# Routing tail and first expert tiles of a chunked-attention and top-2 expert kernel: tile order, copy engines and one-hots rearranged

## The chip, the cores and the metric

The kernel runs on one core of a Trainium2 chip. Its time is the device time of one execution in microseconds (us); a median of several runs stands for it. A core has TensorE (PE: matmuls, and transposes done as matmuls), VectorE (DVE), ScalarE (ACT), GpSimd (POOL) and SyncE (SP). The last two mostly issue DMAs here. The profiler records one execution; "PEld" are TensorE's weight loads, which run beside its matmuls.

## The reference

Attention over chunks of 32 positions, with 16 positions of context to the left, 8 to the right and 8 memory rows, feeds a mixture of 8 experts, of which each token takes its best two.

```python
# q, k, v: (4, 8, 768, 64); mem_k, mem_v: (4, 8, 8, 64)
for c in range(S // 32):
    k_full = concat(mem_k, k[max(0, c0 - 16):min(S, c1 + 8)])
    a = softmax(q[c0:c1] @ k_full.T / 8)
    out[c0:c1] = a @ v_full
x = out as (3072, 512)
noisy = x @ w_gate + log1p(exp(x @ w_noise)) * noise      # (3072, 8)
top2 = the two largest; weights = softmax over these two
out = sum over the two experts e: weight * (relu(x @ w1[e]) @ w2[e])   # F = 1024
```

## The kernel before

The 3072 tokens are 24 groups of 128 (six for each batch). The kernel has three stages.

**Attention** goes batch by batch, two groups at a time: twelve steps `i` (`NT = 12`, `TP = 3` for each batch). Step `i` issues the scores of step `i + 1` (`scores`, L408), turns its own probabilities by TensorE (`turn_p`), multiplies by the values (`values`), turns the result (`turn_x`) and multiplies it by the gate weights (`gate`, L489). `gate` leaves 16 logits for each token in one PSUM tile, `small`, from where they are copied into `lg_all` (L496). Between two batches the queries and keys of the next are turned in eight units of two heads (`turns`, L560). The plan `KS`/`QS` (L570) says for each unit which engine copies PSUM to SBUF: a key unit is two copies, and the unit's number tells how many of the two go to ScalarE, the others going to VectorE. While TensorE would wait, `warm` (L450) gives it matmuls whose results nobody reads.

**Routing** runs beside it in four parts of groups: `r0` (0 to 5), `ra` (6 to 13), `rb` (14 to 19) and `rc` (20 to 23), each an object of `Route` (L239). `noise` makes the noise scale on ScalarE. `choose` is a chain of 14 short VectorE steps that finds the two best experts and ends in `ohp`, a one-hot over the 28 pairs of experts. `ranks` counts by matmul how many earlier tokens have the same pair: a triangle within the group, and matrices of ones for earlier groups and for the running total `cum` of the earlier parts. `place` reads the rank of each token (`ohr`, `rank`), `total` adds the part's counts to `cum` (L330, L334), and `slots` makes the one-hot `oh_l` of the rank over 128 places (L341). `weights` and `values` prepare the facts of each token on GpSimd, and `lists` brings them by matmul to the place of their pair and rank. `decode` then gives `src`, the row to be gathered for each place of each pair.

**Experts**: the rows of each pair form a tile of 128. `gathers` fetches tiles by indirect DMA (L695) into six buffers, in blocks of six or eight tiles. They are turned by TensorE for the first block (`turn_slots`, L715) and by DMA on SP's queue for the others (`turn_dma`, L720). `mm1` multiplies by `w1` (L738) and leaves the relu to ScalarE and VectorE in turn, `mm2` multiplies by `w2` (L752), and the weighted sum goes to the output by indirect DMA. The loads of the experts' weights stand on the same GpSimd queue as the gathers, in the order of the program.

In the attention and routing stage the order on TensorE, ScalarE, VectorE and SP is that of the program (`manual_schedule`), and so it is for TensorE and VectorE at the opening of the expert stage. Everything emitted later is put in by a planner, which may place an instruction between two of those. Waits between engines are derived from tiles; two engines do not read the same PSUM bank of one tile at the same time.

The first step of the expert stage takes three tiles for expert 0. Before, the first of them goes alone, so that TensorE can begin when one tile has landed, and the other two are a pair:

```python
h0 = mm1(xTs[b][:, :, 0:1, :], 1, static_w(e), 0, others)   # others: turn tiles 1 and 2
s0, n = 1, 2
h = mm1(xTs[b][:, :, s0:s0 + (n - 1) * ds_ + 1:ds_, :], n, static_w(e), i % 2)
```

Of the kernel before, what the change touches and what calls it, by code (L numbers as in the profile page):

```python
# [11 lines left out]
F32 = mybir.dt.float32  # L12
# [3 lines left out]
Alu = mybir.AluOpType  # L16
# [6 lines left out]
def kernel(  # L23
# [215 lines left out]
    class Route:  # L239
# [10 lines left out]

        def noise(self):
            self.ns = self.tile("ns", E).rearrange("p (n e) -> p n e", e=E)
            nc.scalar.activation(out=self.ns, in_=self.lg[:, :, E:2 * E], func=Act.Exp)
            nc.scalar.activation(out=self.ns, in_=self.ns, func=Act.Ln, bias=1.0)
# [35 lines left out]

        def ranks(self):
            n, M = self.n, self.M
            self.p_rank = bank([128, n, NP], F32, name="p_rank")
            nc.tensor.matmul(out=self.p_rank, lhsT=tri, rhs=M, start=True, stop=False)
            nc.tensor.matmul(out=self.p_rank, lhsT=ones, rhs=cum[-1].unsqueeze(1).to_broadcast([128, n, NP]),
                             start=False, stop=False)
# [17 lines left out]

        def settle(self):
            yield from self.place()
            yield from self.total()
            self.slots(nc.vector)
            yield
# [16 lines left out]

        def slots(self, eng, parts=1):
            n = self.n // parts
            self.oh_l = self.tile("oh_l", 128, BF16).rearrange("p (n t) -> p n t", t=128)
            for g in range(0, self.n, n):  # L340
                keep_order(eng, eng.tensor_tensor(out=self.oh_l[:, g:g + n], in0=bc(self.rr[:, g:g + n], 128),  # L341
                                                  in1=io_l.unsqueeze(1).to_broadcast([128, n, 128]), op=Alu.is_equal))

# [145 lines left out]
    def gate(t, xT):  # L489
        b, tp = divmod(t, TP)  # L490
        ps_l = small[:, 2 + t % 2, 0:4 * E].rearrange("p (j e) -> p j e", j=2)
        for j in range(2):
            for kp in range(KP):
                nc.tensor.matmul(out=ps_l[:, j, :], lhsT=xT[:, kp, j, :], rhs=wgn[:, kp, :],
                                 start=(kp == 0), stop=(kp == KP - 1))
        nc.vector.tensor_copy(lg_all[:, 2 * t:2 * t + 2, :], ps_l)  # L496

# [32 lines left out]
    with tc.manual_schedule(engines={ET.PE, ET.Activation, ET.DVE, ET.SP}):  # L530
# [38 lines left out]

        KS = ((0, 2), (1, 0), (2, 2), (3, 2))  # L570
        QS = ((4, 1), (5, 1), (6, 1), (7, 1))
# [4 lines left out]
        for i in range(NT):  # L576
# [24 lines left out]
            if tp == TP - 1 and more:  # L601
                home = psO.tile([128, 2, HP, 2, D], F32, name="ps_o")
                waits = lambda pair: warm(home[:, 0].rearrange("p c a d -> p (c a d)"), (0, 4, 0, 1)[pair])
            if not last:
# [19 lines left out]
            if i in (TP + 2, 2 * TP + 2):  # L624
                advance((ra if b > 1 else r0).settle())
            if i in (2 * TP, 3 * TP):
# [7 lines left out]
            if i == 2 * TP + 1:  # L634
                ra.noise()
                advance(ra.choose())
            if i == NT - 2:
                rb.noise()
                chosen = rb.choose()
                advance(chosen, 7)  # L640
            fill(i, 2)

        i = NT - 1
# [159 lines left out]
    wl = next(dec)  # L803
    advance(rc.total())

# [148 lines left out]
    for i, (b, e, s0, ds_, n, ps_) in enumerate(steps):  # L954
        if i == 0:
# [4 lines left out]
            nc.vector.tensor_copy(xTs[0][:, :, 6, :], xTs[0][:, :, 0, :])  # L960
            s0, n = 1, 2
        h = mm1(xTs[b][:, :, s0:s0 + (n - 1) * ds_ + 1:ds_, :], n, static_w(e), i % 2)
        if i == 0:
            turn_slots(0, 3, 1)
            turn_slots(0, 4, 2)
            turn_block(1, 0, 8)
            opening.close()
        if prev is not None:
            second(prev, held=held if i == len(steps) - 1 else None)
        for f in feed.get(i, ()):  # L970
            f()
        tiles = []
# [4 lines left out]
        if i == 0:  # L977
            second((h0, 1, static_w(e), tiles[0:1]))
            tiles = tiles[1:]
        prev = (h, n, static_w(e), tiles)  # L980

        if i == 6:
            inc_ = count()
        if i == 9:
# [83 lines left out]
```

## Time and profile before

| | us |
|---|---|
| median of 3 runs | 347.69 |
| lowest, highest | 346.8, 348.42 |
| the profiled execution | 345.12 |
| its span, first to last instruction | 343.5 |
| TensorE busy (matmuls) | 284.4 |
| VectorE, ScalarE, GpSimd busy | 161.0, 141.0, 135.0 |
| mean granted TensorE clock | 0.921 |

In the rows of the profile a time is counted from the span's start. A row of the timeline gives the start, the busy time, the engine, the line, the operation, the tile written and the tiles read, the shapes (partitions x elements), the count, and in brackets the idle time of the engine before it with what ended it. "SPq" or "POOLq" is the queue of that engine. In a row of windows the last three numbers are the granted clock, the busy share of the 16 DMA engines and GB/s.

### The profile page before, as it was taken

What the parts mean: (1) busy time and instruction counts of PE and PEld (TensorE: products, weight loads), DVE (VectorE), ACT (ScalarE), POOL (GpSimd) and SP (SyncE); (2) the same over time, 40 slices, a digit from 0 to 9 for tenths busy, and PEclk for the clock granted to TensorE, in tenths of its full rate; (3) what the DMA queues carried; (4) which work ended last, traced back from release to release, by engine and by line L of the source; (5) the groups of instructions that cost most, each with busy time, mean ns of one, the idle gap of its engine ahead of it and who ended that gap; (6) DMA issues with size and microseconds to landing.
All of it is one profiled execution on the core that took longest, in us unless ns stands there. A gap on an engine that the chain in (4) does not pass through costs nothing.

```text
span 343.5 us, 7180 instructions
## 1 busy us (share of the span) xinstructions
PE 284.4 (83%) x3001; PEld 177.0 (52%) x3021; DVE 161.0 (47%) x348; ACT 141.0 (41%) x195; POOL 135.0 (39%) x186
## 2 busy tenths in 40 slices
PE   0356484777786868799999999999999999999993
PEld 0355453655655634655544465764446666555542
DVE  7658426769769787411224201964410134313232
ACT  8823656585775610244321343222244321344310
POOL 6460574346480046813831353652381033201123
PEclk9995869787869886999999999999999999999998
DMA  8989999999999992799999999996189992100002
GB/s 120 224 196 186 252 165 213 259 219 235 259 201 241 222 235 60 123 223 194 165 176 202 255 139 214 222 147 150 58 159 172 188 221 94 59 25 4 24 28 105
DMA packets 49818, 56.97 MB, mean 166 GB/s; under 512 B 16883, under 2 KB 39475, under 8 KB 49780
## 3 DMA queue, kind: packets, MB, share of 16 engines
q0 software_dynamic: 34192, 46.82, 75.3%
q1 hardware_dynamic: 13920, 6.62, 11.0%
q10 hardware_dynamic: 1668, 3.02, 2.6%
q8 instruction: 25, 0.41, 0.5%
q14 instruction: 13, 0.11, 0.1%
HBM read 70.39 MB, written 13.76 MB: 245 GB/s over the span
## 4 chain that ended last, share of the span: by engine, by line
PE 46%; DMA 11%; DVE 3%; SPq 3%; POOL 2%; issue 1%; ACT 0%; POOLq 0%; DVEq 0%
PE p_y L752 22%; PE p_h L738 21%; DMA xt<-xd,main_src 6%; DMA xTt<-xt 5%; SPq L720 3%; POOL xt L695 1%; DVE w_all L474 1%; PE p_x L484 0%; POOLq L1063 0%; ACT xT L486 0%; PE p_y L930 0%; PE p_h L910 0%; PE p_p L444 0%; POOL w_all L81 0%; PE p_list L358 0%
## 5 line engine op out<-in xcount | busy, mean ns | idle before, releaser
L738 PE MATMUL p_h<-xTt,w_all 128*128 128x256 bf16 (+3 forms) x669 | 100.5, 308 | 1.2 <-DMA xTt<-xt 0.5
L752 PE MATMUL p_y<-w_all,h 128*128 128x512 bf16 (+1 forms) x439 | 98.8, 375 | 0.9
L738 PEld LDWEIGHTS <-w_all 128*128 128x128 bf16 x672 | 64.0, 98 | 36.0 <-issue 1.6
L726 ACT ACTIVATE h<-p_h 128x512 bf16<-128x512 f32 (+1 forms) x79 | 43.4, 550 | 91.1 <-PE p_h L738 87.8
L752 PEld LDWEIGHTS <-h 128*128 128x128 bf16 x456 | 44.4, 98 | 49.9 <-issue 0.4
L724 DVE TENSOR_SCALAR h<-p_h 128x512 bf16<-128x512 f32 (+1 forms) x47 | 29.6, 630 | 74.4 <-PE p_h L738 67.7
L701 POOL DMA_INDIRECT out_dram<-y,main_dst x28 | 30.9, 1103 | 81.1 <-DVE y L760 68.0
L695 POOL DMA_INDIRECT xt<-xd,main_src x28 | 28.0, 1000 | 28.6 <-DMA xTt<-xt 17.3
L760 DVE SCALAR_TENSOR_TENSOR y<-p_y,main_w,y 128x512 f32<-128x512 f32 (+1 forms) x29 | 21.2, 732 | 38.4 <-PE p_y L752 36.9
L399 PE MATMUL p_t<-identb,w_all 128*64 128x128 bf16 x384 | 19.4, 274 | 23.2 <-DMA w_all<-in_k_dram 14.6
L756 ACT ACTIVATE y<-p_y,main_w 128x512 f32<-128x512 f32 x28 | 19.2, 687 | 36.5 <-PE p_y L752 35.5
L399 PEld LDWEIGHTS <-w_all 128*64 128x64 bf16 x384 | 16.8, 145 | 25.4 <-DMA w_all<-in_k_dram 15.4
L389 POOL DMA_DIRECT2D w_all<-vd x16 | 11.8, 746 | 22.7 <-DMA vd<-vp 17.5
L447 ACT COPY pT<-p_p 128x1024 bf16<-128x1024 bf16 x12 | 12.1, 1010 | 18.3 <-PE p_p L444 18.3
L474 DVE TENSOR_TENSOR w_all<-ps_o,rs 128x512 bf16<-128x512 f32 x24 | 15.5, 686 | 4.2 <-PE ps_o L467 3.3
L438 ACT ACTIVATE pb<-sc 128x1024 bf16<-128x1024 f32 x12 | 12.8, 1063 | 9.3 <-DVE sc L433 9.2
L374 POOL COPY vp<-w_all 128x1536 bf16<-128x1536 bf16 x8 | 11.5, 1467 | 11.5 <-DMA w_all<-in_v_dram 11.5
L563 ACT COPY kT<-p_t 64x768 bf16<-64x768 bf16 x18 | 14.3, 793 | 3.7 <-PE p_t L399 3.5
L433 DVE TENSOR_TENSOR sc<-ps_s,mx 128x1024 f32<-128x1024 f32 x12 | 14.7, 1225 | 0.8
L431 DVE TENSOR_REDUCE mx<-ps_s 128x16 f32<-128x1024 f32 x12 | 14.7, 1222 | 0.8 <-PE ps_s L423 0.5
L486 ACT COPY xT<-p_x 128x1024 bf16<-128x1024 bf16 x12 | 12.2, 1017 | 2.1 <-PE p_x L484 2.1
L423 PE MATMUL ps_s<-kT,qT 128*32 128x112 bf16 x384 | 10.8, 260 | 2.4 <-issue 1.6
(188 smaller groups left out, 284.5 us busy)
## 6 DMA issues: line engine op xcount, KB each, us to landing
w_all<-in_moe_w_dram POOLq DMA_DIRECT2D x16, 1024.0 KB, 19.0
w_all<-in_moe_w_dram POOLq DMA_DIRECT2D x8, 512.0 KB, 12.9
w_all<-in_v_dram POOLq DMA_DIRECT2D x4, 768.0 KB, 11.2
w_all<-in_k_dram POOLq DMA_DIRECT2D x4, 768.0 KB, 16.0
w_all<-in_q_dram POOLq DMA_DIRECT2D x4, 768.0 KB, 16.7
vd<-vp SPq DMA_DIRECT2D x4, 768.0 KB, 8.7
w_all<-vd POOLq DMA_DIRECT2D x8, 384.0 KB, 11.3
w_all<-vd POOLq DMA_DIRECT2D x8, 288.0 KB, 10.5
```

Of the source, the lines that this page charges most:

```text
L399: nc.tensor.transpose(out=p_t[own(par), s, :], in_=src[:, 2 * pair + par, s * D:(s + 1) * D], identity=identb, tile_position=(0, par * 64))
L431: nc.vector.tensor_reduce(out=mx, in_=s3, axis=AX, op=Alu.max)
L433: nc.vector.tensor_tensor(out=sc, in0=s3, in1=bc(mx, KW), op=Alu.subtract)
L474: nc.vector.tensor_tensor(out=xr[:, j, 0:Dm].rearrange("p (h d) -> p h d", h=H), in0=ps_o[:, j].rearrange("p c a d -> p (c a) d"), in1=bc( ...
L695: i = nc.gpsimd.indirect_dma_start(out=xts[key].bitcast(I32), out_offset=None, in_=xd, in_offset=bass.IndirectOffsetOnAxis(ap=ix, axis=0))
L701: i = nc.gpsimd.indirect_dma_start(out=out.rearrange("n (r c) -> (n r) c", r=cuts), out_offset=bass.IndirectOffsetOnAxis(ap=ix, axis=0), i ...
L724: nc.vector.tensor_scalar(out=out_, in0=in_, scalar1=0.0, scalar2=None, op0=Alu.max)
L726: nc.scalar.activation(out=out_, in_=in_, func=Act.Relu)
L738: nc.tensor.matmul(out=o, lhsT=w(kp * F + f * 128, 128), rhs=x[:, kp], start=(kp == 0), stop=(kp == KP - 1))
L752: nc.tensor.matmul(out=p, lhsT=h[:, (f * n + j) * 128:(f * n + j + 1) * 128], rhs=w(KP * F + f * Dm + x * c, c), start=(f == 0), stop=(f = ...
L756: nc.scalar.activation(out=y, in_=ps[0], func=Act.Copy, scale=weight)
L760: nc.vector.scalar_tensor_tensor(out=o, in0=p, scalar=weight, in1=o, op0=Alu.mult, op1=Alu.add)
```

## The change

Six edits go together.

1. At the opening of the expert stage tiles 0, 1 and 2 each get a `mm1` of their own; the transposes of tile 1 stand in the middle of tile 0's, those of tile 2 in the middle of tile 1's, and `mm2` of tiles 0 and 1 follows as soon as their hidden rows are there.
2. Of the key copies between two batches ScalarE makes five instead of six and VectorE three instead of two. The choice of `ra` is issued in two parts, nine steps ahead of the copies and five behind them, and three of the four warm-up matmuls ahead of the second pair's scores are dropped.
3. The totals of `ra`, `rb` and `rc` are emitted in the expert stage (at its step 6). The ranks of `rb` and `rc` therefore take the one-hots of all groups since `r0` by one matmul with ones for each, ahead of the triangle: 9 and 15 matmuls, where `cum` took one. Warm-ups at that place become none instead of 2 and 5 instead of 8.
4. `slots` makes its one-hots with one tensor_scalar for each group, where one tensor_tensor took all or half of the part's groups.
5. The logits of steps 8, 9 and 10 are copied by ScalarE instead of VectorE.
6. The Exp of `rc` is made in two parts: for the two older groups from `lg_all`, for the two newest from PSUM.

```diff
-        def noise(self):
+        def noise(self, fresh=None):
             self.ns = self.tile("ns", E).rearrange("p (n e) -> p n e", e=E)
-            nc.scalar.activation(out=self.ns, in_=self.lg[:, :, E:2 * E], func=Act.Exp)
+            old = self.n if fresh is None else self.n - 2
+            nc.scalar.activation(out=self.ns[:, 0:old], in_=self.lg[:, 0:old, E:2 * E], func=Act.Exp)
+            if fresh is not None:
+                nc.scalar.activation(out=self.ns[:, old:self.n], in_=fresh[:, :, E:2 * E], func=Act.Exp)
...
-        def ranks(self):
+        def ranks_of(self, before):
+            n = self.n
+            self.p_rank = bank([128, n, NP], F32, name="p_rank")
+            rows = [cum[-1]] + [r.M[:, g] for r in before for g in range(r.n)]
+            for x, row in enumerate(rows):
+                nc.tensor.matmul(out=self.p_rank, lhsT=ones, rhs=row.unsqueeze(1).to_broadcast([128, n, NP]),
+                                 start=(x == 0), stop=False)
+
+        def ranks(self, before=()):
             n, M = self.n, self.M
...
-        def settle(self):
+        def settle(self, total):
             yield from self.place()
-            yield from self.total()
+            if total:
+                yield from self.total()
...
-        def slots(self, eng, parts=1):
-            n = self.n // parts
+        def slots(self, eng):
             self.oh_l = self.tile("oh_l", 128, BF16).rearrange("p (n t) -> p n t", t=128)
-            for g in range(0, self.n, n):
-                keep_order(eng, eng.tensor_tensor(out=self.oh_l[:, g:g + n], in0=bc(self.rr[:, g:g + n], 128),
-                                                  in1=io_l.unsqueeze(1).to_broadcast([128, n, 128]), op=Alu.is_equal))
+            for g in range(self.n):
+                keep_order(eng, eng.tensor_scalar(out=self.oh_l[:, g], in0=io_l, scalar1=self.rr[:, g:g + 1], scalar2=None,
+                                                  op0=Alu.is_equal))
...
-        nc.vector.tensor_copy(lg_all[:, 2 * t:2 * t + 2, :], ps_l)
+        (nc.scalar.copy if NT - 4 <= t < NT - 1 else nc.vector.tensor_copy)(lg_all[:, 2 * t:2 * t + 2, :], ps_l)
+        return ps_l
...
-        KS = ((0, 2), (1, 0), (2, 2), (3, 2))
+        KS = ((0, 2), (1, 0), (2, 2), (3, 1))
...
-                waits = lambda pair: warm(home[:, 0].rearrange("p c a d -> p (c a d)"), (0, 4, 0, 1)[pair])
+                waits = lambda pair: warm(home[:, 0].rearrange("p c a d -> p (c a d)"), (0, 1, 0, 1)[pair])
...
-                advance((ra if b > 1 else r0).settle())
+                advance((ra if b > 1 else r0).settle(b == 1))
...
                 ra.noise()
-                advance(ra.choose())
+                chosen = ra.choose()
+                advance(chosen, 9)
...
             fill(i, 2)
+            if i == 2 * TP + 1:
+                advance(chosen)
...
-        warm(p_w, 2)
-        gate(i, xT)
-        rc.noise()
-        rb.ranks()
-        advance(rb.total())
+        rb.ranks_of((ra,))
+        rc.noise(gate(i, xT))
+        rb.ranks(None)
...
-        warm(p_w, 8)
-        rc.ranks()
+        rc.ranks_of((ra, rb))
+        warm(p_w, 5)
+        rc.ranks(None)
...
-        rc.slots(nc.vector, 2)
+        rc.slots(nc.vector)
...
     wl = next(dec)
-    advance(rc.total())
...
         if i == 0:
-            def others():
-                turn_slots(0, 1, 1)
-                turn_slots(0, 2, 1)
-            h0 = mm1(xTs[b][:, :, 0:1, :], 1, static_w(e), 0, others)
-            nc.vector.tensor_copy(xTs[0][:, :, 6, :], xTs[0][:, :, 0, :])
-            s0, n = 1, 2
+            w = static_w(e)
+            h0 = mm1(xTs[b][:, :, 0:1, :], 1, w, 0, lambda: turn_slots(0, 1, 1))
+            h1 = mm1(xTs[b][:, :, 1:2, :], 1, w, 1, lambda: turn_slots(0, 2, 1))
+            nc.vector.tensor_copy(xTs[0][:, :, 6, :], xTs[0][:, :, 0, :])
+            second((h0, 1, w, tiles[0:1]))
+            s0, n = 2, 1
...
         if i == 6:
+            for r in (ra, rb, rc):
+                advance(r.total())
             inc_ = count()
```

More of the change, by code (lines that the diff above doesn't have):

```diff
@@ L289, in choose @@
             yield
-        def ranks(self):
+        def ranks_of(self, before):
[6 more added lines that the diff above has]
+        def ranks(self, before=()):
             n, M = self.n, self.M
[L293 to L296, printed above, removed]
+            if before is not None:
+                self.ranks_of(before)
+            nc.tensor.matmul(out=self.p_rank, lhsT=tri, rhs=M, start=False, stop=False)
             for g in range(n - 1):
@@ L954 @@
     for i, (b, e, s0, ds_, n, ps_) in enumerate(steps):
-        if i == 0:
-            def others():
-                turn_slots(0, 1, 1)
-                turn_slots(0, 2, 1)
-            h0 = mm1(xTs[b][:, :, 0:1, :], 1, static_w(e), 0, others)
-            nc.vector.tensor_copy(xTs[0][:, :, 6, :], xTs[0][:, :, 0, :])
-            s0, n = 1, 2
[L962 to L971, printed above, removed]
         tiles = []
@@ L977 @@
         if i == 0:
-            second((h0, 1, static_w(e), tiles[0:1]))
-            tiles = tiles[1:]
+            w = static_w(e)
[4 more added lines that the diff above has]
+            s0, n = 2, 1
+        h = mm1(xTs[b][:, :, s0:s0 + (n - 1) * ds_ + 1:ds_, :], n, static_w(e), i % 2)
+        if i == 0:
+            turn_slots(0, 3, 1)
+            turn_slots(0, 4, 2)
+            turn_block(1, 0, 8)
+            second((h1, 1, w, tiles[1:2]))
+            tiles = tiles[2:]
+            opening.close()
+        if prev is not None:
+            second(prev, held=held if i == len(steps) - 1 else None)
+        for f in feed.get(i, ()):
+            f()
         prev = (h, n, static_w(e), tiles)
         if i == 6:
+            for r in (ra, rb, rc):
+                advance(r.total())
             inc_ = count()
```

## The prediction

> **What bounds the kernel now.** The page first: its span, its slices of the DMA engines, and the shares of the chain that ended last.
>
> ```profile
> span 343.5 us, 7180 instructions
> ...
> DMA  8989999999999992799999999996189992100002
> ...
> PE 46%; DMA 11%; DVE 3%; SPq 3%; POOL 2%; issue 1%; ACT 0%; POOLq 0%; DVEq 0%
> ```
>
> The execution took 345.12 us, its span 343.5. The runs shown have a median of 347.69, 2.57 above it; I make the sum against the profiled execution and take the difference off the median. Half a per cent, about what the runs can tell from no change, is 1.7 us. Then the chain in order of time (start, length, what):
>
> ```profile
> 116.22 1.29 DVE w_all L474 x2
> ...
> 135.27 4.25 DMA xt<-xd,main_src
> ...
> 145.63 16.72 DMA xt<-xd,main_src
> ...
> 172.01 16.63 DMA xTt<-xt
> ...
> 188.78 5.99 PE p_h L738 x27
> ```
>
> Until 131 us the routing sets the time, nearly one DVE step after another. Then the gathers of the sorted rows and their DMA transposes run to 188.64, and from there TensorE alone. The waits of TensorE agree; the only one in the expert stage's steady part is
>
> ```profile
> PE p_h L738 <- DMA xTt<-xt: 0.5, 1, 0.5
> ```
>
> So a microsecond saved in routing moves everything behind it. One saved by TensorE between 139 and 188 counts only if the last transpose lands earlier too.
>
> **Key copies and the choice.** The timeline where batch 3's keys arrive:
>
> ```profile
> 94.38 1.90 PE L399 MATMUL p_t<-identb,w_all 128*64 128x128 bf16 x36 [2.12 <-DMA w_all<-in_k_dram]
> 95.04 4.84 ACT L563 COPY kT<-p_t 64x768 bf16<-64x768 bf16 x6 [0.19 <-PE p_t L399]
> 95.62 0.22 DVE L258 TENSOR_REDUCE mm<-nl 128x8 f32<-128x64 f32 x1
> 97.15 1.92 DVE L563 COPY kT<-p_t 64x768 bf16<-64x768 bf16 x2
> 98.00 1.89 PE L452 MATMUL ps_o<-identb,ones 128*128 128x512 bf16 x4
> 101.43 0.17 DVE L426 MEMSET ps_s<- 32x128 f32 x1 [2.12 <-PE ps_s L423]
> 101.63 1.23 DVE L431 TENSOR_REDUCE mx<-ps_s 128x16 f32<-128x1024 f32 x1
> ```
>
> TensorE waited 2.12 us for the keys' load, so what earlier batches gain or lose ends at 94.38. ScalarE's copies cost 0.81 each (4.84 / 6). Now it makes five, to 95.04 + 4.03 = 99.07. In the built order DVE's third copy waits for ScalarE's fifth, which reads the same PSUM tile, so it runs to 99.07 + 0.96 = 100.0, no sooner than ScalarE's sixth did (99.88). Behind it in DVE's queue stand the five remaining steps of the choice: from 95.62 to the copies' start at 97.15 is 1.5 us for six steps, so 1.3 for five, and one step more (0.2) brings the MEMSET to 101.5. The scores are ready before: three warm-up matmuls fewer (1.89 / 4 = 0.47 each) let TensorE finish within 0.7 us of the last key. I take zero; the ends are -0.6 (the scores alone decide) and +0.3.
>
> **Totals.** The built order does not take them out of the line. The planner puts `ra`'s in front of and behind the next `mx`, `rb`'s ahead of the last copy of the logits, `rc`'s between `ohr`, `rank` and the one-hots. For `ra` 0.66 us only moves within a stretch where DVE has no idle time, zero (-0.1 to +0.2):
>
> ```profile
> 106.39 0.52 DVE L330 TENSOR_REDUCE red<-ohp 128x28 f32<-128x224 bf16 x1
> ...
> 107.05 1.22 DVE L341 TENSOR_TENSOR oh_l<-rank,io_l 128x1024 bf16<-128x1024 f32 x1
> 108.19 1.22 DVE L431 TENSOR_REDUCE mx<-ps_s 128x16 f32<-128x1024 f32 x1
> ```
>
> **One-hots per group.** No row shows a bf16 tensor_scalar of 128 elements. The nearest, by duration per form (mean ns before the last bar):
>
> ```profile
> L870 DVE TENSOR_SCALAR kt<-key 128x24 f32<-128x24 f32 x1 | 0.5, 459 | 0.0
> L960 DVE COPY xTt<-xTt 128x512 bf16<-128x512 bf16 x1 | 0.3, 282 | 0.0
> L853 DVE TENSOR_SCALAR low<-rank 128x24 f32<-128x24 f32 x1 | 0.2, 170 | 0.0
> ```
>
> The copy is nearest: one bf16 source in SBUF, like `io_l`. With 170 ns for almost no elements it spends some 0.13 us on 512, so 0.03 on 128. Steps without a wait follow each other faster than their durations: in the tail below a copy and the reduction behind it start 0.11 apart. I take 0.1 each; ends 0.1 and 0.46 (L870, the same operation at its slowest). For `ra` eight take 0.8 where the tensor_tensor held DVE 1.14 (107.05 to 108.19): -0.34.
>
> **Logits and the tail.**
>
> ```profile
> 115.75 1.07 ACT L438 ACTIVATE pb<-sc 128x1024 bf16<-128x1024 f32 x1
> ...
> 117.64 0.24 ACT L253 ACTIVATE ns<-lg_all 128x48 f32<-128x48 f32 x1 [0.81 <-DVE lg_all L496]
> 118.19 0.21 DVE L271 TENSOR_TENSOR ns<-ns,nz 128x48 f32<-128x48 f32 x1 [0.58 <-ACT ns L254]
> ...
> 123.55 0.19 DVE L496 COPY lg_all<-small 128x32 f32<-128x32 f32 x1 [0.34 <-PE small L494]
> 123.66 0.43 DVE L330 TENSOR_REDUCE red<-ohp 128x28 f32<-128x168 bf16 x1
> 124.29 0.19 DVE L271 TENSOR_TENSOR ns<-ns,nz 128x32 f32<-128x32 f32 x1
> ...
> 127.88 0.95 DVE L341 TENSOR_TENSOR oh_l<-rank,io_l 128x768 bf16<-128x768 f32 x1
> 128.75 0.26 DVE L323 TENSOR_TENSOR ohr<-ohp,p_rank 128x112 f32<-128x112 bf16 x1
> 129.34 0.76 DVE L341 TENSOR_TENSOR oh_l<-rank,io_l 128x256 bf16<-128x256 f32 x2
> ```
>
> ScalarE is free at 116.82. Copy, Exp and Ln at some 0.25 each end at 117.6, while DVE is busy with `w_all` until 117.51, so the choice starts at 117.62 and not 118.19: -0.57. The next logits copy leaves from between two `w_all` steps: -0.1. Ends of both: 0 and -0.7.
>
> The last copy stays on DVE, and the Exp of the fresh logits waits for it, since both read one PSUM tile; reading PSUM directly saves nothing. `rb`'s total (0.43, and 0.11 for the short sum behind it) now stands ahead of that copy, where DVE waited only 0.34 for TensorE: +0.2 (0 to +0.3). The 24 rank matmuls replace five warm-ups in TensorE's waiting time; its slack is the 1.5 us before `rc`'s choice ends, cost zero.
>
> `rb`'s six one-hots hold DVE 0.6 instead of 0.87 (127.88 to 128.75): -0.27. `rc`'s four take 0.4 instead of 0.76, and TensorE follows one group later instead of two: -0.34. `rc`'s total in that line: two short steps beside waits of 0.3, +0.13 (ends 0 and the 0.52 of a total's rows).
>
> Routing: 0 - 0.34 - 0.57 - 0.1 + 0.2 - 0.27 - 0.34 + 0.13 = **-1.29**.
>
> **The first tiles.**
>
> ```profile
> 136.52 1.05 PE L738 MATMUL p_h<-xTt,w_all 128*128 128x128 bf16 x16 [0.51 <-DVE xTt L716]
> ...
> 139.57 0.40 PE L715 MATMUL p_xt<-identb,xt 128*128 128x128 bf16 x4 [1.78 <-DMA xt<-xd,main_src]
> 139.81 4.55 PE L738 MATMUL p_h<-xTt,w_all 128*128 128x128 bf16 x48
> ```
>
> Sixteen 128-wide matmuls take 1.05 us, so tiles 1 and 2 alone cost 4 x 1.05 = 4.20 where the 32 paired ones cost 4.55 - 1.05 = 3.50: +0.70. The third gather lands at 139.52; TensorE now has 2.1 us of other matmuls from 137.8 on and reaches it at 139.9, so the idle 1.78 goes. Together **-1.08** (+0.70 if the gather then lands later, -1.78 if wide and narrow cost alike). What is late next: the transposes of block 1.
>
> ```profile
> 159.23 0.96 POOL L695 DMA_INDIRECT xt<-xd,main_src  x1 [11.26 <-DMA xTt<-xt]
> ...
> 163.00 0.95 POOL L695 DMA_INDIRECT xt<-xd,main_src  x1 [0.30 <-issue]
> ```
>
> ```profile
> L720 SPq DMA_TRANSPOSE xTt<-xt x2: 1200/1256/1313, 149.5 to 150.9; - x2
> ...
> DMA to landing us min/median/max: 11.2/11.2/11.2
> ```
>
> The changed order reuses gather buffers otherwise. Block 1's fourth gather now waits, on POOL's queue, for the first transpose (159.23), the fifth for the second, which lands at 150.9 + 11.2 = 162.1; before, the last gather alone needed that one. So the eighth goes out at 162.1 + 3 x 1.26 = 165.9 instead of 163.0, and expert 4's load behind it as much later. Before, SP's last transpose started at 172.01, held back by DMA and not by its gather, and took 16.63 beside the loads of experts 4 and 5. With those 2.9 us later the transposes have the DMA engines longer to themselves. TensorE arrives at 188.25 - 1.29 - 1.08 = 185.9, so the landing must come 1.5 us earlier than routing alone moves it. At a third of the engines beside loads (my estimate from 5 transposes and 3 loads in those 16.63 us) 2.9 us alone are worth more than that. Then the wait of **-0.53** goes as well. The loads have time: TensorE waits for none after 188.
>
> Sum: -1.29 - 1.08 - 0.53 = -2.9: 342.2 beside the profiled 345.12, **344.8** beside the median.
>
> **Rivals.**
>
> *The landing still binds.* For it: the chain runs through it, and later gathers can only delay it. Against it: SP was held by DMA, not by gathers. If it moves with routing alone, the gain is 1.29: 346.4. If the 2.9 us go through in full, 188.64 + 2.9 - 1.29 = 190.3: +1.5, 349.2.
>
> *The one-hots are dear (slower).* L870 took 0.46 where L853 took 0.17, with GpSimd issuing DMAs at the time. The 18 one-hots of `ra`, `rb` and `rc` at 0.46 cost 18 x 0.36 = 6.5 more than my 0.1: +3.6, 351.3. The forecast is lost from 0.26 each and slower by half a per cent from 0.36. For it: GpSimd multiplies `vals` just beside the last ten. Against it: at 107 GpSimd is idle, and L960 was not slowed. [...]
>
> *The clock.* The granted clock (third number from the end) before and after the warm-ups:
>
> ```profile
> 98.00:101.50 3.50, 3.50 (x40) 1.33 (x37) 1.33 (x4) 1.84 (x3) 3.03 (x8) 0.50 1.10 196
> 101.50:105.00 3.50, 2.84 (x85) 2.52 (x86) 3.33 (x6) 2.78 (x3) 1.43 (x1) 1.00 1.14 207
> ```
>
> A stretch with TensorE busy throughout was followed by full clock. Three warm-ups fewer leave 1.4 us of it idle; at half clock the next 2.84 us of work could take 5.7, some 1.5 of it beyond DVE's 3.5 and the slack: 346.3. [...] Against the rival: the idle gaps stay short.
>
> **How the numbers follow.** Forecast 0.50 (its own range 343.2 to 346.0: below, the first tiles at -1.8, the keys at -0.6 and the scatter of the runs; above, the one-hots at 0.15 each and the keys at +0.3); the landing 0.22; the one-hots 0.20; the clock 0.08. Faster 0.50, same 0.22 + 0.08 = 0.30, slower 0.20. The range goes from 343.2 to 349.5, over both ends of the landing and the one-hots up to 0.36.
>
> **What would show it.** Right: one-hots that start 0.1 apart; the choice of `rb` starting without a logits copy on DVE ahead of it; the first gather at 130.8 instead of 132.06; no wait for gathers between TensorE's first and third tile; no wait for `xTt` in the 128x512 steps. Wrong: a wait there as long as the gain ahead of it, one-hots of 0.2 or more, or half clock behind 101.5 or 135.6.

## The result, and the profile after

The changed kernel takes 350.50 us (median of 16 runs) where the kernel before takes 347.54 (median of 16): the ratio is 1.0075, 95% interval 1.0051 to 1.0099. I forecast 344.8 and faster; it is slower by some 2.6 us, and 350.5 lies above my range. All ratios leave out the runs that fell in a slower state of the chip, two of the sixteen here. The profiled execution took 350.37 us.

The page of the changed kernel, its span, DMA slices and shares of the chain, and then four pieces of the chain in order of time (start, length, what):

```profile
span 348.7 us, 7305 instructions
...
DMA  8989999999999981599899999996179993100002
...
PE 60%; DVE 4%; issue 1%; POOLq 0%; ACT 0%; POOL 0%; DVEq 0%
```

```profile
118.98 1.29 DVE w_all L484 x2
...
138.65 1.72 issue
...
141.27 1.05 PE p_h L751 x16
...
187.22 5.18 PE p_y L765 x24
```

In this profile gathers and transposes, 11% of the chain before, have gone from it: from 141.27 on it is nearly all TensorE's own work. That is what the change to the first tiles promised. (In a second profile of the changed kernel, experiment 16, they are back with 9% of the chain, and TensorE waits 0.6 us for a transpose.) But the stage starts late. The first gather goes out at 135.12 and not at 132.06, and the first expert matmul starts at 141.27 and not at 136.52.

To see where that comes from I cut the time at `mx`, VectorE's maximum over the scores, of which each batch has three. Each entry is the difference of two times in one profile (us), of two starts except in the last row; both kernels were profiled twice.

| stretch | before | before, again | changed | changed, again |
|---|---|---|---|---|
| last `mx` of batch 1 to first of batch 2 | 11.51 | 11.66 | 13.43 | 13.63 |
| first to last `mx` of batch 2 | 11.78 | 12.32 | 10.99 | 11.42 |
| last of batch 2 to first of batch 3 | 13.29 | 13.24 | 13.96 | 14.37 |
| first to second `mx` of batch 3 | 6.56 | 6.56 | 6.87 | 6.88 |
| second to third | 4.95 | 5.18 | 5.52 | 5.52 |
| third `mx` to the first gather | 18.92 | 18.79 | 19.66 | 19.38 |
| first gather to first expert matmul | 4.46 | 4.35 | 6.15 | 4.39 |
| first expert matmul to TensorE's end | 201.12 | 203.75 | 201.34 | 199.36 |

The largest loss, 1.9 us, stands in the first row, in batch 2, where my prediction had not looked at all. Batch 2 gives back 0.8 of it; the four rows from the last `mx` of batch 2 to the first gather together lose 2.3. Of these, the row from the second to the third `mx` stays open: it took 5.51 in experiments 9 and 11 too, which have the one-hots as before, and 4.58 in experiment 13, which has the new ones. The last row shows a gain of some 2, and also how far one execution can be from the next: the profile I predicted from was 2.6 us shorter there than the second profile of the same kernel.

**Batch 2.** VectorE and GpSimd of the changed kernel there, then of the kernel before (timeline: start, length, engine, line, what, idle before it and who ended it):

```profile
74.50 0.96 DVE L574 COPY kT<-p_t 64x768 bf16<-64x768 bf16 x1 [1.51 <-ACT kT L574]
75.50 2.34 DVE L323 TENSOR_TENSOR facts<-ii 128x6 bf16<-128x6 f32 x1
77.92 0.17 DVE L436 MEMSET ps_s<- 32x128 f32 x1
78.12 1.23 DVE L441 TENSOR_REDUCE mx<-ps_s 128x16 f32<-128x1024 f32 x1
```

```profile
74.92 2.88 POOL L384 COPY vp<-w_all 128x1536 bf16<-128x1536 bf16 x2
```

```profile
73.24 0.18 DVE L313 TENSOR_TENSOR facts<-ii 128x6 bf16<-128x6 f32 x1
76.36 0.17 DVE L426 MEMSET ps_s<- 32x128 f32 x1 [2.94 <-PE ps_s L423]
76.56 1.23 DVE L431 TENSOR_REDUCE mx<-ps_s 128x16 f32<-128x1024 f32 x1
```

```profile
75.33 2.88 POOL L374 COPY vp<-w_all 128x1536 bf16<-128x1536 bf16 x2
```

The step that writes `facts` compares six columns. It took 0.18 us at 73.24, two microseconds before GpSimd began its copies. In the changed kernel it stands behind the third key copy, which waits 1.51 us for ScalarE, starts at 75.50, half a microsecond after GpSimd, and ends at 77.84. GpSimd's copies end at 77.80. The step was not slow, it was held. The MEMSET and `mx` stand behind it in VectorE's queue; TensorE's last matmul of their scores had ended at 75.95.

**Batch 3.** The same kind of row comes back, here with a total:

```profile
100.02 0.96 DVE L574 COPY kT<-p_t 64x768 bf16<-64x768 bf16 x1 [1.13 <-ACT kT L574]
...
102.56 0.17 DVE L436 MEMSET ps_s<- 32x128 f32 x1
102.64 0.40 DVE L341 TENSOR_REDUCE red<-ohp 128x28 f32<-128x224 bf16 x1
103.07 1.22 DVE L441 TENSOR_REDUCE mx<-ps_s 128x16 f32<-128x1024 f32 x1
104.21 0.89 DVE L345 TENSOR_TENSOR cum<-cum,red 128x28 bf16<-128x28 bf16 x1
105.02 1.21 DVE L443 TENSOR_TENSOR sc<-ps_s,mx 128x1024 f32<-128x1024 f32 x1
```

```profile
102.62 2.44 POOL L358 TENSOR_TENSOR vals<-ohp,facts 128x1344 bf16<-128x1344 bf16 x1 [2.60 <-DVE facts L323]
```

Before, `cum` came after GpSimd's `vals` had ended:

```profile
106.94 0.19 DVE L334 TENSOR_TENSOR cum<-cum,red 128x28 bf16<-128x28 bf16 x1
```

```profile
100.49 2.44 POOL L348 TENSOR_TENSOR vals<-ohp,facts 128x1344 bf16<-128x1344 bf16 x1
```

`cum`, 28 columns, 0.19 us there, now ends at 105.10; `vals` ends at 105.06. While `vals` ran, `red` (one input, 0.40 us; 0.52 before) and `mx` (reading PSUM, 1.22) were not held. In the second profile of the changed kernel the two held steps are there again:

```profile
75.99 1.93 DVE L323 TENSOR_TENSOR facts<-ii 128x6 bf16<-128x6 f32 x1
...
105.13 0.90 DVE L345 TENSOR_TENSOR cum<-cum,red 128x28 bf16<-128x28 bf16 x1
```

**Who is held.** Of the steps that were held, each is the one that started second: `facts` starts 0.58 us after `vp` and ends 0.04 behind it, `cum` 1.59 after `vals` and ends 0.04 behind that. The other direction is in the kernel before. There VectorE's wide one-hots of `rb` started at 127.88 (quoted in the prediction), and GpSimd's `vals`, which started 0.16 later, took 1.21 us; in the changed kernel the same instruction, started at 130.58, takes 0.56. First before, then changed:

```profile
128.04 1.21 POOL L348 TENSOR_TENSOR vals<-ohp,facts 128x224 bf16<-128x224 bf16 x1 [0.20 <-DVE ohp L288]
```

```profile
130.58 0.56 POOL L358 TENSOR_TENSOR vals<-ohp,facts 128x224 bf16<-128x224 bf16 x1 [0.20 <-DVE ohp L291]
```

What the two held steps of VectorE share is their inputs. `facts` (2.34 and 1.93 us in the two profiles, 0.18 before) and `cum` (0.89 and 0.90, 0.19 before) have two, both in SBUF, and the `vp` and `vals` that they waited out read SBUF; beside `vals`, `red` with one input and `mx` from PSUM were not held. That the inputs decide it is my reading of these few rows, and no run changes the inputs alone. (A one-hot per group, below, has one tensor input and was held too, for 0.61 us; why, no run here shows.)

### The profile page after: what moved, and what is told of

Read it like the earlier page. It is cut to its first block, busy times and chain, and to the rows that moved or that the text cites. A ratio compares the mean times of both kernels' runs of the same rounds, so it can differ in the third digit from the quotient of the medians.

```text
span 348.7 us, 7305 instructions
## 1 busy us (share of the span) xinstructions
PE 287.0 (82%) x3061; PEld 182.2 (52%) x3061; DVE 167.9 (48%) x368; ACT 138.0 (40%) x195; POOL 134.1 (38%) x186
## 4 chain that ended last, share of the span: by engine, by line
PE 60%; DVE 4%; issue 1%; POOLq 0%; ACT 0%; POOL 0%; DVEq 0%
PE p_h L751 28%; PE p_y L765 28%; PE p_list L368 1%; DVE w_all L484 1%; PE ps_s L462 0%; DVE oh_l L351 0%; PE p_xt L728 0%; POOLq L1076 0%; PE p_y L942 0%; PE p_h L922 0%; PE p_p L454 0%; PE ps_o L477 0%; DVE vals L358 0%; DVE xTt L729 0%; PE ps_s L433 0%
## 5 line engine op out<-in xcount | busy, mean ns | idle before, releaser
L765 PE MATMUL p_y<-w_all,h 128*128 128x512 bf16 (+1 forms) x456 | 100.5, 375 | 1.4 <-ACT y L769 1.4
L751 PEld LDWEIGHTS <-w_all 128*128 128x128 bf16 x704 | 64.8, 98 | 36.3 <-issue 1.9
L739 ACT ACTIVATE h<-p_h 128x512 bf16<-128x512 f32 (+1 forms) x78 | 42.7, 549 | 91.8 <-PE p_h L751 82.9
L737 DVE TENSOR_SCALAR h<-p_h 128x512 bf16<-128x512 f32 (+1 forms) x48 | 30.3, 631 | 73.7 <-PE p_h L751 60.3
L574 DVE COPY kT<-p_t 64x768 bf16<-64x768 bf16 x9 | 8.6, 956 | 12.2 <-PE p_t L409 8.0
L433 PE MATMUL ps_s<-kT,qT 128*32 128x112 bf16 x384 | 11.5, 275 | 3.1 <-DVE kT L574 2.9
L574 ACT COPY kT<-p_t 64x768 bf16<-64x768 bf16 x15 | 11.9, 792 | 3.8 <-PE p_t L409 3.6
```

The lines of the kernel that those rows point to most:

```text
L574: (nc.scalar.copy if eng > part else nc.vector.tensor_copy)(o_, i_)
L737: nc.vector.tensor_scalar(out=out_, in0=in_, scalar1=0.0, scalar2=None, op0=Alu.max)
L739: nc.scalar.activation(out=out_, in_=in_, func=Act.Relu)
L751: nc.tensor.matmul(out=o, lhsT=w(kp * F + f * 128, 128), rhs=x[:, kp], start=(kp == 0), stop=(kp == KP - 1))
L765: nc.tensor.matmul(out=p, lhsT=h[:, (f * n + j) * 128:(f * n + j + 1) * 128], rhs=w(KP * F + f * Dm + x * c, c), start=(f == 0), stop=(f = ...
```

## Experiments

All ratios are against the kernel before on the same chip, with 95% intervals; 0.1% is 0.35 us.

**1. The keys alone** (before, with the key edits).

```
-        KS = ((0, 2), (1, 0), (2, 2), (3, 2))
+        KS = ((0, 2), (1, 0), (2, 2), (3, 1))
...
-                waits = lambda pair: warm(..., (0, 4, 0, 1)[pair])
+                waits = lambda pair: warm(..., (0, 1, 0, 1)[pair])
...
-                advance(ra.choose())
+                chosen = ra.choose()
+                advance(chosen, 9)
...
+            if i == 2 * TP + 1:
+                advance(chosen)
```

> The kernel before with only the key edits: the last unit's second half copied by VectorE (5:3), three warm-up matmuls fewer, the choice of ra in two pieces. Theory A (the third VectorE copy is late, and what queues behind it meets GpSimd): the copy starts about 1.5 us after the second one ended in each batch; in batch 2 the step writing facts then stands behind GpSimd's copies of vp and takes over 2 us instead of 0.18, so mx of batch 2 starts 1.5 us later than 76.6; at the start of batch 3 mx is 1 to 1.5 us later than 101.6; the whole is 1 to 2 us slower (349). Theory B (the keys cost nothing, the loss is in the first tiles): within 0.5 us of the kernel before.

Measured: 1.0067 (1.0038 to 1.0097), 2.3 us slower, a little more than theory A's 1 to 2. Its place is the one that theory A named. VectorE of this run, then GpSimd:

```profile
75.45 1.65 DVE L313 TENSOR_TENSOR facts<-ii 128x6 bf16<-128x6 f32 x1
77.18 0.17 DVE L426 MEMSET ps_s<- 32x128 f32 x1
```

```profile
74.18 2.88 POOL L374 COPY vp<-w_all 128x1536 bf16<-128x1536 bf16 x2
```

`facts` ends at 77.10, GpSimd at 77.06. This `mx` comes 13.01 us after the last of batch 1, against 11.51 and 11.66. The 1 to 1.5 us that I expected at the start of batch 3 did not show in this profile: 101.1 there, no later than 101.6. Nor does this one profile show how the held step becomes 2.3 us of the whole: its first gather goes out 66.48 us after the last `mx` of batch 1, where the kernel before took 67.01 and 67.75, and what is long in it is the expert stage (205.87). Experiment 9 is what ties the loss to `facts`.

**2. The first tiles alone** (before, with the new loop body for step 0).

```
...
-            h0 = mm1(xTs[b][:, :, 0:1, :], 1, static_w(e), 0, others)
...
-            s0, n = 1, 2
...
+            h0 = mm1(xTs[b][:, :, 0:1, :], 1, w, 0, lambda: turn_slots(0, 1, 1))
+            h1 = mm1(xTs[b][:, :, 1:2, :], 1, w, 1, lambda: turn_slots(0, 2, 1))
...
+            second((h0, 1, w, tiles[0:1]))
+            s0, n = 2, 1
...
```

> The kernel before with only the first tiles visited one by one. Theory A: the wait of 1.78 us for the third gather goes, the extra narrow matmuls cost 0.7, and tile 1 waits some 0.5 us for VectorE's copy of xTt: 0 to 1 us faster (347). Theory B (this part carries the loss): tile 1's wait for xTt is 1.1 us or more, block 1's gathers wait longer, and it is 1.5 to 2.5 us slower (349.5).

Measured: 0.9942 (0.9917 to 0.9967), 2.0 us faster, beyond theory A's gain. It does not show in single profiles: from the first expert matmul to TensorE's end this run took 201.55, the profile I predicted from 201.12. Over all profiles it does: the nine with tiles 1 and 2 as a pair took 200.12 to 206.24, mean 203.35; the nine with the tiles one by one 198.56 to 204.79, mean 201.07. Part of the difference is the clock. Between 140 and 147 the granted clock fell to 0.77 or less in four of the nine with the pair (experiments 1, 3, 6 and 10), and in one of the nine without (experiment 5, 0.57). Experiment 1 is the clearest; TensorE's 32 two-tile matmuls there (6.57 us), beside those of experiment 4 (3.65 us), and the window of the keys' run (PEclk is the third number from the end):

```profile
140.37 6.57 PE L741 MATMUL p_h<-xTt,w_all 128*128 128x256 bf16 x32 [2.10 <-issue]
```

```profile
139.04 3.65 PE L741 MATMUL p_h<-xTt,w_all 128*128 128x256 bf16 x32 [0.87 <-issue]
```

```profile
140.00:143.00 3.00, 2.63 (x13) 1.83 (x13) 1.38 (x3) 0.60 (x1) 2.61 (x3) 0.50 0.74 112
```

**3. The one-hots alone** (before, with a tensor_scalar per group).

```
...
-                keep_order(eng, eng.tensor_tensor(out=self.oh_l[:, g:g + n], ...
+                keep_order(eng, eng.tensor_scalar(out=self.oh_l[:, g], in0=io_l, scalar1=self.rr[:, g:g + 1], ...
```

> The kernel before with only the one-hots made per group. Theory A: they follow each other 0.17 us apart, 0.22 beside GpSimd's multiplication, so ra gains nothing (1.3 against 1.14), rb loses 0.4 (1.3 against 0.87), rc nothing: 0.2 to 0.8 us slower (348). Theory B (as I predicted, 0.1 apart): 0.9 us faster. If each took 0.46: 3.6 slower.

Measured: 1.0014 (0.9981 to 1.0046): no gain, and my 0.9 us faster lies outside (0.9974). The interval does not tell 0 from theory A's loss. The tile's view and two rows of the timeline of the changed kernel have the reason:

```profile
L351 DVE TENSOR_SCALAR oh_l<-io_l,rank x24: 241/247/610, 83.3 to 133.0; 128x128 bf16<-128x128 bf16 x24
```

```profile
108.64 1.39 DVE L351 TENSOR_SCALAR oh_l<-io_l,rank 128x128 bf16<-128x128 bf16 x8
109.94 1.22 DVE L441 TENSOR_REDUCE mx<-ps_s 128x16 f32<-128x1024 f32 x1
...
130.42 1.42 DVE L351 TENSOR_SCALAR oh_l<-io_l,rank 128x128 bf16<-128x128 bf16 x6
```

Eight hold VectorE from 108.64 to 109.94, 0.163 us each, where the one wide step before held it 1.14. Of the six at 130.42 the second takes 0.61: it started at 130.58 with GpSimd's `vals` and ended at 131.19, 0.05 behind it. With the new form the six need 1.34 us and not 0.87.

**4. The logits alone** (before, with ScalarE's copies and the fresh Exp).

```
...
-        nc.vector.tensor_copy(lg_all[:, 2 * t:2 * t + 2, :], ps_l)
+        (nc.scalar.copy if NT - 4 <= t < NT - 1 else nc.vector.tensor_copy)(lg_all[:, 2 * t:2 * t + 2, :], ps_l)
```

> The kernel before with only the logits of the last steps copied by ScalarE and the last Exp reading PSUM. Both theories: the choice of rb starts as soon as VectorE's w_all steps end, 0.4 to 0.7 us faster (347); a rival (ScalarE's copies push pb or xT back): no change, with the gap moved to a wait for pT or xT.

Measured: 0.9985 (0.9957 to 1.0012). The size fits, the interval includes no change. The stretch from the third `mx` to the first gather shrinks to 18.21, where the five profiles with this part of the routing as before (the kernel before twice, experiments 1, 2 and 9) took 18.59 to 18.92, and the changed kernel has the mechanism: `rb`'s choice starts as `w_all` ends, with no logits copy between.

```profile
118.98 1.29 DVE L484 TENSOR_TENSOR w_all<-ps_o,rs 128x512 bf16<-128x512 f32 x2 [0.55 <-PE ps_o L477]
120.19 0.20 DVE L274 TENSOR_TENSOR ns<-ns,nz 128x48 f32<-128x48 f32 x1
```

**5. The changed kernel without the keys** (the diff of experiment 1, undone).

> The changed kernel with the key edits undone (ScalarE copies six of the eight key halves again, all warm-up matmuls, the choice of ra unbroken). If the keys carry the loss as the run of the keys alone says: 2.3 us or more faster than the changed kernel, so 347 to 348 here, level with the kernel before. If moved totals carry a loss of their own, 348 to 349. If all of the loss needed the keys (the collision of cum with GpSimd's vals starts only when the keys are late): 346.

Measured: 1.0014 (0.9988 to 1.0039). The keys' 0.6% is in the changed kernel too. What is left is level with the kernel before although the first tiles gain, so something else loses, as far as the interval can tell.

**6. The totals as moved, alone** (before, with `ranks_of`, `settle(total)` and the totals after step 6).

> The kernel before with only the totals' edits (rank matmuls over the earlier groups' one-hots, totals left to the planner). Theory A (the planner puts them back into the line, and cum, which reads two SBUF tiles, waits for GpSimd's multiplication to end): cum of rb takes 0.6 instead of 0.2, the last logits copy comes 0.4 to 0.6 us later, red and cum of rc add 0.3: 0.5 to 1 us slower. Theory B (they only move): within 0.3 us.

Measured: 1.0021 (0.9993 to 1.0048), 0.7 us, with `cum` of `rb` held for 0.61; the interval includes no change. Here, and in experiment 5, `ra`'s `cum` still runs ahead of GpSimd's `vals` (0.19 us); it is the late keys that put it beside it.

**7. The changed kernel with the totals really out** (tied behind the copy that duplicates the first tile; the planner cannot put them earlier).

```
-            nc.vector.tensor_copy(xTs[0][:, :, 6, :], xTs[0][:, :, 0, :])
+            cp = nc.vector.tensor_copy(xTs[0][:, :, 6, :], xTs[0][:, :, 0, :])
...
-            for r in (ra, rb, rc):
-                advance(r.total())
+            with tc.issue_after(cp.ins):
+                for r in (ra, rb, rc):
+                    advance(r.total())
```

> The changed kernel with the three totals tied behind the copy that duplicates the first tile, so that they really leave the routing's line. Theory A: 1.5 us faster than the changed kernel (red and cum at the start of batch 3 held VectorE 1.3 us, those of rb 1.0, those of rc 0.3, some of it hidden): 349. Theory B (they cost nothing where they were): 350.5.

Measured: 1.0023 (0.9994 to 1.0052) against the changed kernel's 1.0075: 1.8 us, the intervals just touching. The stretch from the first to the second `mx` of batch 3 falls from 6.87 and 6.88 to 6.20, that from the third to the gather from 19.66 and 19.38 to 18.64.

**8. First tiles and logits together.**

> The kernel before with the two edits that alone did not lose: first tiles one by one, and the logits of the last steps copied by ScalarE. If they add: 0.9927 of the kernel before, 345.0 or a little less. If the logits' gain is used up by the wait for a gather: 345.4, as with the first tiles alone.

Measured: 0.9956 (0.9926 to 0.9987). It does not tell whether the logits add anything to the first tiles.

**9. The keys, with `facts` ahead of the key copies** (experiment 1 and one step moved).

```
             if i == TP + 1:
                 advance(chosen)
+                r0.order()
...
                 r0.weights(nc.gpsimd)
-                r0.order()
```

> The kernel before with the key edits of the first run and one step moved: VectorE's step that writes facts of r0 in batch 2 stands ahead of the key copies and not behind the third. If half of the keys' loss is that this step meets GpSimd's copies of vp (1.65 and 2.3 us instead of 0.18): the start of batch 2's mx comes 0.8 us or more earlier relative to the last mx of batch 1 than the 13.0 us of the keys' run, and the loss shrinks from 2.3 to some 1 us (348.8). If the late third copy alone sets it: no change against the keys' run (349.7), since mx waits for the scores of that copy.

Measured: 0.9987 (0.9956 to 1.0017) against 1.0067: not half but all of the keys' loss has gone. VectorE and GpSimd of this run:

```profile
69.95 0.17 DVE L313 TENSOR_TENSOR facts<-ii 128x6 bf16<-128x6 f32 x1
...
73.78 0.96 DVE L563 COPY kT<-p_t 64x768 bf16<-64x768 bf16 x1 [1.81 <-ACT kT L563]
75.33 0.17 DVE L426 MEMSET ps_s<- 32x128 f32 x1 [0.59 <-PE ps_s L423]
```

```profile
74.31 2.88 POOL L374 COPY vp<-w_all 128x1536 bf16<-128x1536 bf16 x2
```

The third copy waits as long as before, GpSimd copies at the same time, and the MEMSET now waits for the scores and for nothing else. The late copy itself costs nothing that the ratio can tell; the small step behind it did.

All profiles together agree on the place. From the last `mx` of batch 1 to the first of batch 2 the five with the late copy and `facts` behind it (the changed kernel twice, experiments 1, 7 and 10) took 12.88 to 13.77; the two with `facts` ahead (9 and 13) 11.28 and 11.39; the eleven with the keys as before 11.13 to 11.86. From the same `mx` to the first gather the same three groups took 68.76 to 71.20 (but experiment 1 66.48), 65.19 and 67.47, and 65.24 to 68.31.

**10. The changed kernel with tiles 1 and 2 as a pair again** (experiment 2, undone).

> The changed kernel with the first tiles visited as before, tiles 1 and 2 together. If the first tiles gain what they gain alone (2.0 us), wherever the routing ends: 2 us slower than the changed kernel, 352.5. If they gain only against the waits of the kernel before: as the changed kernel, 350.5.

Measured: 1.0106 (1.0071 to 1.0141) against 1.0075: 1.1 us slower, between the two expectations; the intervals overlap.

**11. The kept parts**: the changed kernel with keys and one-hots undone and the totals out as in experiment 7.

> The changed kernel with the keys and the one-hots undone and the totals tied behind the first tile's copy: what is left is the first tiles one by one, the logits by ScalarE and the totals really out of the line. If the parts add: first tiles -0.6%, logits -0.15%, totals out of the line some -0.1 to -0.3%: 0.990 of the kernel before, 344.2. If first tiles alone hold all the gain: 345.4.

Measured: 0.9884 (0.9855 to 0.9914), 1.2% faster than the kernel before, and faster than each part (the medians, 340.44 and 345.71 us, would give 1.5%). TensorE's waits from 128 us to the end are these, without one for a gather or a transpose of gathered rows:

```profile
PE p_xt L726 <- ACT main_w L532: 0.9, 1, 0.9
PE p_h L749 <- DVE xTt L727: 0.5, 1, 0.5
PE p_list L369 <- DVE vals L359: 0.2, 1, 0.2
```

**12 and 16. Both kernels once more, for their profiles.**

> The kernel before once more, for its profile alone: from TensorE's first expert matmul to its last it took 201.1 us in the profile I predicted from, while the three variants with the same expert stage took 202.9 to 206.2. If that profile was a fortunate one, this takes 203 us or more, with a stretch at half clock behind the first tiles; if the variants' own edits lengthen it, 201.

> The changed kernel once more, for its profile. If the longer wait for the first gather belongs to it: 6.1 to 6.4 us again from the first gather's issue to the first expert matmul. If it belonged to that one execution: 4.4, as in the others.

Measured: 203.75 us in the expert stage of the kernel before, so the 201.12 of the profile I had was a fortunate one. But the half clock behind the first tiles that I expected is not there: the granted clock was 1.00 from 136 to 190. The wait for `xTt`, 0.53 before, was 2.13 (to 189.98), the clock from 190 to 200 was 0.83 instead of 1.00, and the 31 matmuls behind the wait took 8.75 instead of 7.07. For the changed kernel 4.39 us from the first gather to the first matmul: the 6.15 belonged to that execution, though experiment 10 had 6.36. What made it so in those two I cannot say.

**13. The changed kernel with both collisions taken out**: `facts` ahead as in 9, totals out as in 7; keys, one-hots, logits and first tiles as changed.

> The changed kernel with two steps moved and nothing else: facts of r0 ahead of the key copies, and the three totals tied behind the first tile's copy. If these two collisions are all of its loss: 0.67 + 0.5 per cent faster than the changed kernel's 1.0075, so 0.995 or 0.996 of the kernel before. If something else in the changed kernel costs (the one-hots, the late keys): 1.000 or above.

Measured: 0.9944 (0.9908 to 0.9980), as expected. With `facts` and the totals moved, the change gains where it lost without. Part of that is no collision undone: the totals out of the line gain by themselves (experiment 15).

**14. The kept parts with the one-hots per group.**

> The run of the kept parts with the one-hots per group put back: it differs from that run (0.988) by the one-hots alone. If they cost only their issue spacing beside GpSimd (0.4 to 0.6 us in rb): 0.990. If they cost 1 us or more (the stretch from the second to the third mx of batch 3 took 5.5 us in every profile with them and 4.6 to 5.2 in all but two without): 0.992 or above.

Measured: 0.9896 (0.9861 to 0.9932) against 0.9884. The one-hots cost nothing that these runs can tell, and gain nothing.

**15. The totals out of the line, alone** (before, with 6 and the edit of 7).

> The kernel before with the totals tied behind the first tile's copy, and nothing else. If being really out of the line is worth what the profiles show (0.5 us at the start of batch 3, 0.3 to 0.6 in rb and rc, and no red and cum ahead of the first tiles' copies): 0.995 to 0.997. If it is worth nothing without the logits edit: 1.000.

Measured: 0.9960 (0.9931 to 0.9988), 1.4 us faster, where the same totals left to the planner were 0.7 slower. First tiles (-0.58%), logits (-0.15) and totals out (-0.40) add to -1.13, and experiment 11 had -1.16; each of these has an interval of about 0.3 either way, so that the agreement is closer than it could be trusted to be.

## Why the prediction was wrong

**Key copies: predicted 0 (-0.6 to +0.3), measured +2.3 us. This is the step that failed**, and in two places. I priced only batch 3, though the edit changes every batch's copies; "what earlier batches gain or lose ends at 94.38" was to cover the rest. In batch 2 the third copy keeps `facts` waiting in VectorE's queue until GpSimd is at its copies (experiments 1 and 9). And in the changed kernel the cover did not hold. The 2.12 us by which TensorE waited for the keys was TensorE's slack; ScalarE, whose copies come next, had only the 0.19 in its own row, which I had quoted. In the changed kernel TensorE no longer waits for the keys' load in either profile (2.12 and 0.92 in the two of the kernel before), and ScalarE's key copies start at 95.95 and 96.87, against 95.04 and 95.64:

```profile
95.95 4.04 ACT L574 COPY kT<-p_t 64x768 bf16<-64x768 bf16 x5
```

In experiment 1 TensorE still waited 1.26 for the load and the copies started at 94.29, so that there the cover held. Within batch 3 the step was right: from the end of the third copy (100.98) to the MEMSET I had 1.5 us, and it is 1.58.

**Totals: predicted +0.33 (0, +0.2, +0.13); measured +0.7 alone (experiment 6, -0.2 to +1.7).** The size cannot be called wrong. The 1.8 us of experiment 7 is not the price of the move: it compares with totals out of the line altogether, which alone gain 1.4 (experiment 15), and the difference is 0.4. What I had wrong is the mechanism. I saw that the built order did not take them out, but priced a moved step at its old duration. `ra`'s `cum` was to move for nothing; beside `vals` it takes 0.89, and `red` and `cum` now stand on either side of `mx`, ahead of `sc`. `rb`'s was held as well:

```profile
125.62 0.60 DVE L345 TENSOR_TENSOR cum<-cum,red 128x28 bf16<-128x28 bf16 x1
...
126.14 0.18 DVE L506 COPY lg_all<-small 128x32 f32<-128x32 f32 x1
```

```profile
125.43 0.75 POOL L358 TENSOR_TENSOR vals<-ohp,facts 128x336 bf16<-128x336 bf16 x1
```

**One-hots: predicted -0.95, measured no gain** (experiments 3 and 14). The term was mis-sized: 0.163 us from one to the next, not 0.1, which I had read from a different pair of steps, a copy and the reduction behind it; and one held for 0.61. The rival (0.46 each, 351.3) had the time of the result nearly right by the wrong steps.

**Logits: predicted -0.67, right as far as it can be told**: the place is right, the stretch 0.4 to 0.7 shorter, the ratio 0.9985.

**First tiles with the wait for `xTt`: predicted -1.08 - 0.53, measured -2.0 alone (-2.9 to -1.1), so right as far as it can be told.** The idle before the third gather went, and gathers took the order I gave; GpSimd's queue of the changed kernel:

```profile
162.19 1.01 POOL L708 DMA_INDIRECT xt<-xd,main_src  x1 [12.48 <-DMA xTt<-xt]
165.71 0.95 POOL L708 DMA_INDIRECT xt<-xd,main_src  x1 [2.51 <-DMA xTt<-xt]
```

The fourth gather waits for one transpose and the fifth for the second, as forecast. TensorE's waits of the changed kernel from 134 us on hold none for `xTt` out of a DMA in the first profile and one of 0.6 us in the second. So "the landing still binds" did not come about in the one, and by little in the other. What I missed is that tile 1 can wait for VectorE's copy of `xTt` (1.1 us in the first profile, two of whose waits follow; none in the second), and that what the pair costs differs from one execution to the next: stretches at half clock in some profiles (0.50 from 140 to 143 in experiment 1), and in the second profile of the kernel before the wait of 2.13 with slow matmuls behind it.

```profile
PE p_xt L728 <- issue: 1.7, 1, 1.7
PE p_h L751 <- DVE xTt L729: 1.6, 2, 1.1
```

**The chances.** Slower had 0.20, all of it on the one-hots. Only for them had I asked what GpSimd is doing at the time. What mattered was the same question for `facts` (2.34 us instead of 0.18) and `cum` (0.89 instead of 0.19), and neither had been listed as a step whose time depends on it. Nor do the two rows I took for the one-hots show it: `L853`, which took 0.17, ran at 134.1 beside a gather issued by GpSimd too (133.97 to 134.97), and why `L870` took 0.46 is open.

**The clock.** This rival had 0.08, and its sign came: in the first profile of the changed kernel the granted clock was 0.50 from 101.5 to 105 and from 135.6 to 139, where it had been 1.00 and 0.99. It is not what made the kernel slow. The second profile had 1.00 from 98 to 105, and the rows there are no shorter (14.37 and 6.88). Experiment 13 had 0.50 from 70 to 80 and from 98 to 105, and its rows are as short as before or shorter (11.39, 13.25, 6.19). Behind 139 TensorE waited for the first tile in any case.

**Summed up** (us, from single ratios): keys +2.3, totals +0.7, one-hots +0.5, logits -0.5, first tiles -2.0 alone, -1.1 in the changed kernel. That is +1.0 to +1.9, against 2.6 measured. Each term is uncertain by about 1 us, and they need not add: `ra`'s `cum` meets `vals` only when the keys are late. The keys are the only term that alone is clear of noise on the losing side.

## What to carry to other kernels

When a step waits longer than before, list what stands behind it in its engine's queue, in every repetition of the loop and not only where the change was meant to act, and look up what GpSimd runs at the new time: here `facts` took 0.18 us by itself and 2.34 behind GpSimd's copies, `cum` 0.19 by itself and 0.89 beside `vals`. A wait on one engine is slack for that engine only; the next engine's slack is in its own row. And "moved out of the line" has to be read from the built order: the same totals gained nothing where the planner put them (+0.2%, not clear of noise) and 0.4% where a dependency held them back.

## What the runs showed of the hardware

A VectorE step was held through more than one GpSimd instruction: `facts`, from 75.50 to 77.84, sat through two copies that follow each other without a gap (74.92 to 76.40 and on to 77.80). The held `facts` and `cum` ended 0.04 us behind the instruction that held them (77.84 and 77.80, 105.10 and 105.06, and 77.10 and 77.06 in experiment 1).

The granted clock of the same stretch of the same code differs between executions: from 101.5 to 105 the changed kernel had 0.50 in one profile and 1.00 in the other. The two profiles of the kernel before differ by 2.6 us in the expert stage, more than most terms of my sum, so one profile was too little to add them up on.

In the first profile of the changed kernel ScalarE and VectorE started on the first tiles' results only at 144.06 and 144.07. The transposes and matmuls of TensorE that they waited for are recorded as ended at 142.55 and 143.44, and they waited for nothing else. Whether the records or the release are late there was not settled.
